# Attention and MoE in one kernel: Q and K of the first two batches loaded on 64 partitions each and transposed together

## The chip, the cores and the metric

One core of one Trainium2 chip. The metric is the device time of one execution in microseconds (us); lower is better. The engines are called PE (TensorE, the matrix unit), PEld (its weight loads), DVE (VectorE), ACT (ScalarE), POOL (GpSimd) and SP (SyncE, which here only issues DMAs). Sixteen DMA engines move data between HBM and SBUF.

## What is computed

Blockwise causal attention over 8 batches of 8 heads, 576 tokens, head size 64; its output, laid out as 4608 rows of 512, goes through a two-layer network with a swish whose steepness is learned per column. All inputs and outputs are float32.

```python
def _attn_ref(q, k, v):                     # q, k, v: (8, 8, 576, 64)
    scores = scale * np.matmul(q, k.transpose(0, 1, 3, 2))
    mask = block_i >= block_j               # blocks of 64 tokens
    scores = np.where(mask, scores, -1000000000.0)
    scores = scores - np.max(scores, axis=-1, keepdims=True)
    attn = np.exp(scores)
    attn = attn / (np.sum(attn, axis=-1, keepdims=True) + 1e-09)
    return np.matmul(attn, v)

def _moe_ref(x, w_in, w_out, beta):         # x: (4608, 512), w_in: (512, 2048), w_out: (2048, 512)
    h = x @ w_in
    g = h * (1.0 / (1.0 + np.exp(-beta * h)))
    return g @ w_out
```

## The kernel before

**Attention.** The work goes in pairs of heads, four pairs a batch; pair `u` of 32 is `b, c = divmod(u, 4)`. For a pair, Q and K are loaded as float32 into a staging tile ST, cast to bf16 into QKn, and turned so that head size lies on partitions (tile QKT: 64 partitions a head). Scores come on PE with keys on partitions (line 712), in four groups of key blocks `g0` 0 to 3: groups 0 to 2 fill two PSUM banks each and take one exponential of 128x1024 on ACT (line 728), group 3 one of 128x64 (line 740). DVE writes zeros over masked corners (734, 736). PE multiplies by V (line 768, 30 small products a pair; V carries a column of ones, so the sum of a row comes out too), DVE takes the reciprocal (780) and scales (787; for pair 1 ACT does it, line 792, in ten pieces). The result is transposed (817) and copied into xT (DVE 827, or ACT 825 for pairs 2 and 3), which is the left operand of the MoE.

**Loads of batches 0 and 1** (`b < QB`). Here Q and K of a pair are two separate loads (line 622) of 96 partitions with six tokens each: 192 pieces of 1536 bytes. There are six staging slots, so three pairs fit. Each load has a cast of its own on POOL, two of sixteen on DVE (629), six transposes of 96x128 (638) and a DVE copy out of PSUM (646). From batch 2 on other loads, casts (669) and DMA transposes (676) are used.

**V.** Batch 0's V is loaded in two halves of four heads. The first half goes by SP into a float32 tile Vs, and POOL casts it into Vn (578). Of the second half SP loads 256 tokens and POOL casts those; the other 320 tokens POOL loads itself by DMAs that cast on the way into Vn (lines 552 and 555). V of batch 1 goes whole through SP into a tile that shares its memory with OV.

**MoE.** Rows go in nine chunks of 512 (`r`). For each of 16 column blocks `j` PE forms h (line 1004, four products of 128x512), ACT takes a tanh (1014) and DVE forms the gated value gT (1018). Chunk 0 multiplies by w_out directly (1040); the others use a Strassen-like scheme (925, combined on DVE in 869 and 889, taken out in 946 and 949). w_in comes in four loads of 512 columns, w_out in four of 512 rows, all issued by POOL and cast on the way (502, 507). The first w_in waits for the K of pair 0, the other three for V of batch 0, w_out for V of batch 1.

**Order.** Nothing is ordered by hand. Every operation is declared with `P.op(engine, duration, emit, deps, tiles, prio, ...)`, and `Plan.schedule` plays the program through with these durations, gives slots of the tile classes and PSUM banks, and fixes the order on every engine by priority (lower goes first). Each engine then runs its list in that order, waiting on semaphores. A DMA has `xfer`, its time on the DMA engines in ns, and `pkt`, the time of one piece, by which two queues share. Where PE has nothing ready, filler products (443, 526) are put in. The loads by SP are chained in one sequence `seq`. `JOIN` lists batches whose pairs are scored two at a time in three visits of PE; other batches have one visit per entry of `GROUPS`.

Of the kernel before, what the change touches and what calls it, by code (L numbers as in the profile page):

```python
# [359 lines left out]
def bass_blockwise_causal_attn__then__act_swish_beta_kernel(  # L360
# [10 lines left out]
    with es:  # L371
        def sb(name, shape, dt):
            return es.enter_context(nc.sbuf_tensor(name, shape, dt))

        NQ = 2
        QB, XB, CAST = 2, 3, "POOL"
        NE = 3
        PARTS = [((0, 4, "SP", (4, 5, 0, 1, 2, 3)), (4, 8, "SP", range(2)), (4, 8, "POOL", (4, 5, 2, 3)))] + [((0, 8, "SP", range(6)),)] * 7
        GROUPS = [((0,), (1,), (2,), (3,))] + [((0, 1), (2, 3))] * 7
        NS = 6  # L380
        JOIN = (2,3,4,5,6,7)
        NO = 4
# [11 lines left out]
        QKn = [sb(f"QKn{i}", [128, 2, 2, 768], bf16) for i in range(NQ)]  # L394
        Vn = [sb(f"Vn{i}", [128, 5, 8, 66], bf16) for i in range(NQ)]
# [206 lines left out]
        xt = []  # L602
        early6 = []
        QKI, QKX = 550, 2700
        for u in range(NU):
# [8 lines left out]
            if b < QB:  # L614

                turned = []
                for w, (nm, src) in enumerate((("Q", q), ("K", k))):
                    ts, pt = P.tile("ST"), P.tile("P1")
                    early6.append(ts)
# [8 lines left out]
                    def fn(g, e, ts=ts, tn=tn, p=p, w=w):  # L628
                        return g.tensor_copy(QKn[tn.slot][0:96, p, w, :].rearrange("p (j h d) -> p j h d", j=6, h=2),  # L629
                                             ST6[ts.slot].rearrange("p h j d -> p j h d"))  # L630
# [5 lines left out]
                    def ft(g, e, tn=tn, pt=pt, p=p, w=w):  # L636
                        for i in range(6):
                            z = g.transpose(PSb[:, pt.slot, 96 * i:96 * i + 96],  # L638
                                            QKn[tn.slot][0:96, p, w, 128 * i:128 * i + 128], identB[0:96, 0:96])
                        return z  # L640

                    o = P.op("PE", 6 * 43, ft, deps=[o, c4], tiles=[tn, pt, tt_], lat=6 * 43 + 170, mode="full",
                             prio=pr(u))

                    def fc(g, e, pt=pt, td=tt_, p=p, w=w):
                        return g.tensor_copy(QKT[td.slot][:, p, w, 0:576].rearrange("c (p j) -> c p j", j=6),
                                             PSb[:, pt.slot, 0:576].rearrange("c (j p) -> c p j", j=6))
# [76 lines left out]
            for g0 in range(4):  # L724
                o, ps = qk[g0]
                if g0 < 3:
                    def fe(g, e, ps=ps, g0=g0, te=te):
                        return g.activation(E3[es_(te)][:, g0, :, :], PS[:, ps.slot:ps.slot + 2, :], ACT.Exp,  # L728
                                            scale=0.125)
                    x = P.op("ACT", act_t(1024), fe, deps=[o], tiles=[ps, te], lat=act_t(1024) + 93, prio=0)  # L730

                    def fz(g, e, g0=g0, te=te):
                        if g0 < 2:
                            return g.memset(E3[es_(te)][64:128, g0, :, 0:64], 0.0)  # L734
                        a = E3[es_(te)][64:128, 2, :, 0:64]
                        return g.memset(bass.AP(a.tensor, a.offset, [a.ap[0], [512, 2], [320, 2], [1, 64]]), 0.0)
                    zs.append(P.op("DVE", 160 if g0 < 2 else 220, fz, deps=[x], tiles=[te], prio=-20))
                else:
                    def fe(g, e, ps=ps, te=te, p=p):
                        return g.activation(E4[es_(te)][:], PS[:, ps.slot, 64 * p:64 * p + 64], ACT.Exp, scale=0.125)  # L740
                    x = P.op("ACT", act_t(64), fe, deps=[o], tiles=[ps, te], lat=act_t(64) + 93, prio=0)
                ex.append(x)
# [38 lines left out]

            r = P.op("DVE", 150, fr, deps=[av], tiles=[pv, ti], prio=0)

# [11 lines left out]

            if u in (1,):
                m = P.op("ACT", 1500, fa, deps=[av, r], tiles=[pv, ti, tx], lat=1700, prio=0)
            else:
                m = P.op("DVE", dve_t(640), fm, deps=[av, r], tiles=[pv, ti, tx], prio=0)
                m.same = [r]  # L800
# [19 lines left out]
            xp = P.op("PE", 5 * 66, fx, deps=nrm, tiles=[tx, px], lat=5 * 66 + 170, mode="full", prio=pr(u)+.5 + 5 * (b < 1))  # L820

# [21 lines left out]
        for b in range(B):  # L843
            for u in range(4 * b, 4 * b + 4):
                for o in (ld["Q", u], ld["K", u]):
                    if o not in seq:
# [287 lines left out]
```

## Time and profile before

| | us |
|---|---|
| median of three runs | 333.79 (333.38 to 335.41) |
| the profiled execution | 331.63 |
| its span, first to last instruction | 329.8 |
| PE busy in the span | 318.9 |
| DVE, ACT, POOL busy | 223.9, 212.6, 87.1 |
| granted PE clock | 1.00 |

A line of a group or timeline names the start or count, the line of the kernel, the engine, the operation and the tiles; in brackets stands how long the engine was idle before it and what released it. The span is also given in 40 slices of 8.2 us, with a digit for the busy tenths. PE's busy time includes filler.

### The profile page before, as it was taken

The numbers are of one execution on the slowest core, as the hardware profiler recorded it, in microseconds if no ns is written. First come the engines' busy times: TensorE is split into PE (matmuls) and PEld (weight loads), VectorE is DVE, ScalarE is ACT, GpSimd is POOL, SyncE is SP. The second block draws the span as 40 slices with busy tenths as digits, with TensorE's granted clock in tenths as the row PEclk, the third lists the DMA queues.
The fourth block names the chain that finished last, engine by engine and source line by source line (L and its number), as shares of the span: only waits on it lengthen the run. The fifth ranks groups of instructions, "written<-read, shape, count | busy, mean of one in ns | idle before, by whom it ended". The sixth has DMA issues, their size and how long they took to land.

```text
span 329.8 us, 7390 instructions
## 1 busy us (share of the span) xinstructions
PE 318.9 (97%) x3111; PEld 198.2 (60%) x3003; DVE 223.9 (68%) x448; ACT 212.6 (64%) x324; POOL 87.1 (26%) x127
## 2 busy tenths in 40 slices
PE   7999999999999999999999998999999999999996
PEld 1364455445687457855666655576566766666685
DVE  4848875678654899449957795678477685666742
ACT  2876974397557976678577675974876554544521
POOL 7756181065073045104530730250000000000000
PEclk9999999999999999999999999999999999999999
DMA  8999999999999999989989999969002320100023
GB/s 206 229 243 236 192 218 205 215 275 196 209 276 190 246 198 189 230 178 203 188 188 191 264 223 151 219 121 165 33 34 42 98 39 32 66 32 34 6 92 127
DMA packets 154993, 53.41 MB, mean 162 GB/s; under 512 B 139072, under 2 KB 154448, under 8 KB 154960
## 3 DMA queue, kind: packets, MB, share of 16 engines
q1 hardware_dynamic: 141200, 40.19, 64.5%
q0 software_dynamic: 5568, 4.36, 8.5%
q10 hardware_dynamic: 8192, 8.39, 8.0%
q8 instruction: 24, 0.39, 0.5%
q14 instruction: 9, 0.07, 0.1%
HBM read 36.71 MB, written 9.44 MB: 140 GB/s over the span
## 4 chain that ended last, share of the span: by engine, by line
PE 83%; ACT 4%; DVE 3%; POOL 3%; SPq 2%; DMA 2%; issue 2%; POOLq 0%; ACTq 0%
PE PS L1004 36%; PE PS L925 28%; PE PS L768 8%; PE PS L712 6%; PE PS L1040 4%; ACT E L728 3%; DMA Vs<-in_v_dram 2%; SPq L552 2%; DVE gT L1018 1%; POOL QKn L629 1%; ACT th L1014 1%; PE PS L817 1%; DVE OV L889 1%; PE PS L638 0%; POOL w_in L502 0%
## 5 line engine op out<-in xcount | busy, mean ns | idle before, releaser
L1014 ACT ACTIVATE th<-PS,beta 128x512 f32<-128x512 f32 x144 | 96.5, 700 | 60.3 <-PE PS L1004 59.1
L1004 PE MATMUL PS<-xT,w_in 128*128 128x512 bf16 x542 | 130.2, 379 | 3.7 <-ACT E L728 1.2
L1018 DVE SCALAR_TENSOR_TENSOR gT<-th,PS 128x512 f16<-128x512 f32 x144 | 95.1, 682 | 30.2 <-ACT th L1014 29.3
L728 ACT ACTIVATE E<-PS 128x1024 bf16<-128x1024 f32 x93 | 92.1, 1029 | 26.1 <-PE PS L712 25.7
L1004 PEld LDWEIGHTS PS<-xT,w_in 128*128 128x128 bf16 x576 | 53.2, 98 | 56.9 <-DVE gT L1018 2.5
L925 PE MATMUL PS<-w_out,gT 128*128 128x256 f16 x512 | 63.0, 273 | 0.0
L925 PEld LDWEIGHTS PS<-w_out,gT 128*128 128x128 f16 x512 | 49.0, 98 | 12.2 <-issue 1.5
L578 POOL CAST Vn<-Vs 128x640 bf16<-128x640 f32 (+1 forms) x28 | 22.4, 800 | 97.4 <-DMA Vs<-in_v_dram 96.1
L669 POOL CAST QKn<-ST 128x640 bf16<-128x640 f32 x48 | 37.9, 790 | 23.7 <-DMA ST<-in_q_dram 13.8
L712 PE MATMUL PS<-QKT 64*128 64x512 bf16 (+4 forms) x328 | 33.8, 295 | 0.4 <-ACT E L740 0.2
L768 PEld LDWEIGHTS PS<-Vn,E 128*128 128x128 bf16 x930 | 31.0, 97 | 4.3 <-issue 0.4
L946 ACT ACTIVATE ost<-PS 128x512 f32<-128x512 f32 x32 | 19.4, 606 | 21.7 <-PE PS L925 21.7
L925 PE MATMUL PS<-OV 128*128 128x256 f16 x256 | 32.0, 273 | 0.5 <-DVE OV L889 0.5
L768 PE MATMUL PS<-Vn,E 128*128 128x65 bf16 x930 | 32.0, 193 | 0.3 <-POOL Vn L578 0.3
L712 PEld LDWEIGHTS PS<-QKT 64*128 64x128 bf16 (+1 forms) x328 | 13.3, 96 | 27.0 <-issue 7.8
L925 PEld LDWEIGHTS PS<-OV 128*128 128x128 f16 x256 | 24.1, 98 | 6.5 <-issue 0.8
L787 DVE TENSOR_TENSOR xq<-PS,inv 128x640 bf16<-128x640 f32 x30 | 24.7, 822 | 0.8
L889 DVE TENSOR_TENSOR OV<-gT 128x1024 f16<-128x1024 f16 x32 | 24.0, 757 | 1.1 <-PE PS L925 0.6
L734 DVE MEMSET E<- 64x64 uint32 x62 | 6.9, 112 | 20.5 <-ACT E L728 18.3
L949 DVE SCALAR_TENSOR_TENSOR ost<-PS,ost 128x512 f32<-128x512 f32 x22 | 15.2, 689 | 8.2 <-PE PS L925 5.8
L925 PE MATMUL PS<-OV,gT 128*128 128x256 f16 x128 | 16.1, 273 | 0.0
L1040 PE MATMUL PS<-w_out,gT 128*128 128x512 f16 x64 | 15.5, 380 | 0.0
(64 smaller groups left out, 175.3 us busy)
## 6 DMA issues: line engine op xcount, KB each, us to landing
out_dram<-ost ACTq DMA_DIRECT2D x32, 256.0 KB, 2.9
ST<-in_q_dram SPq DMA_DIRECT2D x12, 576.0 KB, 6.2
ST<-in_k_dram SPq DMA_DIRECT2D x12, 576.0 KB, 7.6
Vs<-in_v_dram SPq DMA_DIRECT2D x24, 256.0 KB, 4.5
ST<-in_q_dram SPq DMA_DIRECT2D x8, 288.0 KB, 6.5
ST<-in_k_dram SPq DMA_DIRECT2D x8, 288.0 KB, 7.0
w_in<-in_moe_w_in_dram POOLq DMA_DIRECT2D x4, 512.0 KB, 10.1
w_out<-in_moe_w_out_dram POOLq DMA_DIRECT2D x4, 512.0 KB, 9.9
```

Of the source, the lines that this page charges most:

```text
L578: return g.tensor_copy(Vn[t.slot][:, 0:n, g0:g1, 0:64], Vs[ts.slot][:, 0:n, g0:g1, :])
L669: return g.tensor_copy(QKn[tn.slot][:].rearrange("p a w n -> p (a w n)")[:, 640 * (2 * a + w):][:, 0:640] .rearrange("p (t h d) -> p t h d ...
L712: z = g.matmul(o, QKT[tqk.slot][r, uu % 2, 1, 128 * t + y:128 * t + m + y], x)
L728: return g.activation(E3[es_(te)][:, g0, :, :], PS[:, ps.slot:ps.slot + 2, :], ACT.Exp, scale=0.125)
L768: z = g.matmul(o, eblk(te, t, i, h), Vn[Tv.slot][:, t, 2 * c + h, 0:65], start=(t == 0), stop=(t == i))
L787: return g.tensor_tensor(xq[xq_(tx)][:].rearrange("p i (h d) -> p h i d", h=2), both(pv, 0, 64), x, ALU.mult)
L889: return P.op("DVE", dve_t(SZ * HC / 2), mk(lambda g: g.tensor_tensor(fo(), fx(), fy(), op)), deps=deps, tiles=tiles, prio=prio)
L925: x = g.matmul(PS[:, pw.slot, HM * w:HM * w + HM], fa()[:, j, 128 * w:128 * w + 128], fb()[:, j, :], start=first and (pair or w == 0) and ...
L1004: z = g.matmul(PS[:, ph.slot, :], w_in[:, c, 128 * j:128 * j + 128], xT[:, c, row % RX:row % RX + RC], start=(c == 0), stop=(c == 3))
L1014: return g.activation(th[tt.slot][:], PS[:, ph.slot, :], ACT.Tanh, scale=beta[:, j:j + 1])
L1018: return g.scalar_tensor_tensor(out=gT[tg.slot][:, j, :], in0=th[tt.slot][:], scalar=1.0, in1=PS[:, ph.slot, :], op0=ALU.add, op1=ALU.mult)
L1040: z = g.matmul(PS[:, po.slot, 0:d1 - d0], gT[tg.slot][:, j, 128 * w:128 * w + 128], w_out[:, j, d0:d1], start=(j == 0), stop=(j == NJ - 1))
```

## The change

It concerns batches 0 and 1, apart from the last item.

- Q and K of a pair share one staging slot: Q on partitions 0 to 63, K on 64 to 127, nine tokens a partition, so 128 pieces of 2304 bytes a load. There are four slots, one a pair. K of pair 0 is issued by ACT, all others by SP.
- One cast covers Q and K of some token columns. For pairs 0 to 3 it is split over engines (`EARLYC`): pair 0 over DVE, ACT and POOL, the others over POOL (five of nine columns) and DVE (four). For batch 1 POOL casts all nine (1152 elements).
- A pair has nine transposes of 128x128 in two PSUM tiles (four and five) with one copy each, by DVE, except the second of pair 0 by ACT.
- All of batch 0's V comes through SP and is cast by POOL.
- The first w_in waits for K of pair 3 rather than of pair 0; the other three wait for the second half of V.
- Batch 1 joins the batches whose pairs are scored two at a time.
- DVE scales pair 1 too; some priorities of batch 0 are changed; the fifth transpose of the attention output takes 128 rows instead of 64.

```diff
-        PARTS = [((0, 4, "SP", (4, 5, 0, 1, 2, 3)), (4, 8, "SP", range(2)), (4, 8, "POOL", (4, 5, 2, 3)))] + [((0, 8, "SP", range(6)),)] * 7
+        PARTS = [((0, 4, "SP", (4, 5, 0, 1, 2, 3)), (4, 8, "SP", (4, 5, 0, 1, 2, 3)))] + [((0, 8, "SP", range(6)),)] * 7
-        NS = 6
-        JOIN = (2,3,4,5,6,7)
+        NS = 4
+        JOIN = range(1, B)
-        ST6 = [s[0:96].rearrange("p t d -> p (t d)")[:, 768 * i:768 * i + 768].rearrange("p (h j d) -> p h j d", h=2, j=6)
-               for s in ST for i in range(3)]
+        ST9 = [s[:, 18 * i:18 * i + 18].rearrange("p t d -> p (t d)") for s in ST for i in range(2)]
...
+        ACTK, QX = (0,), 745
+        EARLYC = {0: (((0, 4), 'DVE'), ((4, 7), 'ACT'), ((7, 9), 'POOL')), 1: (((0, 5), 'POOL'), ((5, 9), 'DVE')), 2: (((0, 5), 'POOL'), ((5, 9), 'DVE')), 3: (((0, 5), 'POOL'), ((5, 9), 'DVE'))}
+        LATEC = (((0, 9), 'POOL'),)
...
-                    def fl(g, e, ts=ts, src=src, b=b, c=c):
-                        return [g.dma_start(ST6[ts.slot].rearrange("p h j d -> p h (j d)"),
-                                            src[b, 2 * c:2 * c + 2].rearrange("h (p j) d -> p h (j d)", j=6))]
-                    o = ld[nm, u] = P.op("SP", 420, fl, tiles=[ts], xfer=1170, prio=u, dma=["d_S", 0, 1])
-                    o.pkt = 80.0
+                    def fl(g, e, ts=ts, src=src, b=b, c=c, w=w):
+                        return [g.dma_start(ST9[ts.slot][64 * w:64 * w + 64].rearrange("p (h n) -> p h n", h=2),
+                                            src[b, 2 * c:2 * c + 2].rearrange("h (p j) d -> p h (j d)", j=9))]
+                    e = "ACT" if w and u in ACTK else "SP"
+                    o = ld[nm, u] = P.op(e, 420, fl, tiles=[ts], xfer=QX, prio=u if e == "SP" else -80,
+                                         dma=["d_SK" if w else "d_S", 0, 1])
+                    o.pkt = 93.0
...
-                    onp = u not in (0, 3) or w == 1
-                    o = P.op("POOL" if onp else "DVE", 850 if onp else 750, fn, deps=[o], tiles=[ts, tn],
-                             prio=-40 + 3 * u if onp else -1)
+                cols = EARLYC[u] if u in EARLYC else LATEC
+                for (j0, j1), en in cols:
...
+                    n = 128 * (j1 - j0)
+                    cast[j0, j1] = P.op(en, 50 + n if en == "POOL" else 60 + 0.65 * n if en == "DVE" else act_t(n), fn, deps=got, tiles=[ts, tn],
+                                        prio=-40 + 3 * u if en == "POOL" else -1 if en == "DVE" else -60)
...
-                        for i in range(6):
-                            z = g.transpose(PSb[:, pt.slot, 96 * i:96 * i + 96],
-                                            QKn[tn.slot][0:96, p, w, 128 * i:128 * i + 128], identB[0:96, 0:96])
+                for a, (j0, j1) in enumerate(((0, 4), (4, 9))):
...
+                        for j in range(j0, j1):
+                            z = g.transpose(PSb[:, pt.slot, 128 * (j - j0):128 * (j - j0) + 128],
+                                            x[:, 128 * j:128 * j + 128], identB[:])
...
-                    turned.append(P.op("DVE", dve_t(576), fc, deps=[o], tiles=[pt, tt_], prio=-5 if b < 1 else .5))
+                    en = "ACT" if u == 0 and a else "DVE"
+                    turned.append(P.op(en, dve_t(128 * n) if en == "DVE" else act_t(128 * n), fc, deps=[o], tiles=[pt, tt_],
+                                       prio=-50 if en == "ACT" else -5 if b < 1 else .5))
...
-            if u in (1,):
+            if u in ():
                 m = P.op("ACT", 1500, fa, deps=[av, r], tiles=[pv, ti, tx], lat=1700, prio=0)
...
-                    r = 128 if i < 4 else 64
-                    z = g.transpose(PSb[:, px.slot, 128 * i:128 * i + r], xq[xq_(tx)][0:r, i, :], identB[0:r, 0:r])
+                    z = g.transpose(PSb[:, px.slot, 128 * i:128 * i + 128], xq[xq_(tx)][:, i, :], identB[:])
...
-        win[0].deps += [ld["K", 0]]
-        for o in ld["VP", 0, 4]:
-            o.deps += [ld["K", 2]]
+        win[0].deps += [ld["K", 3]]
         for w in win[1:]:
-            w.deps += ld["V", 0, 4] + (ld["VP", 0, 4] if w is not win[1] else [])
+            w.deps += ld["V", 0, 4]
```

The exponentials of batch 0 get priority -2 instead of 0, its reciprocals and scalings -6 instead of 0.

More of the change, by code (lines that the diff above doesn't have):

```diff
@@ L393, in bass_blockwise_causal_attn__then__act_swish_beta_kernel @@
         SW = {k: OVh[:, k + 1] for k in (2, 3)}
-        QKn = [sb(f"QKn{i}", [128, 2, 2, 768], bf16) for i in range(NQ)]
+        QKn = [sb(f"QKn{i}", [128, 2, 2, 640], bf16) for i in range(NQ)]
         Vn = [sb(f"Vn{i}", [128, 5, 8, 66], bf16) for i in range(NQ)]
@@ L614, in bass_blockwise_causal_attn__then__act_swish_beta_kernel @@
             if b < QB:
[L616 removed]
+                turned, got, cast = [], [], {}
+                ts, pts = P.tile("ST"), [P.tile("P1"), P.tile("P1")]
+                early6.append(ts)
                 for w, (nm, src) in enumerate((("Q", q), ("K", k))):
[L618 to L647 removed]
@@ new lines, in bass_blockwise_causal_attn__then__act_swish_beta_kernel, with fn @@
+                    o.pkt = 93.0
+                    got.append(o)
+                cols = EARLYC[u] if u in EARLYC else LATEC
+                for (j0, j1), en in cols:
+                    def fn(g, e, ts=ts, tn=tn, p=p, j0=j0, j1=j1):
+                        y = QKn[tn.slot][:].rearrange("p a w n -> p (a w n)")[:, 1152 * p:1152 * p + 1152].rearrange(
+                            "p (j h d) -> p j h d", h=2, j=9)[:, j0:j1]
+                        x = ST9[ts.slot].rearrange("p (h j d) -> p j h d", h=2, j=9)[:, j0:j1]
+                        if e == "ACT":
+                            return g.activation(y, x, ACT.Copy)
+                        return g.tensor_copy(y, x)
+                    n = 128 * (j1 - j0)
+                    cast[j0, j1] = P.op(en, 50 + n if en == "POOL" else 60 + 0.65 * n if en == "DVE" else act_t(n), fn, deps=got, tiles=[ts, tn],
+                                        prio=-40 + 3 * u if en == "POOL" else -1 if en == "DVE" else -60)
@@ new lines, in bass_blockwise_causal_attn__then__act_swish_beta_kernel, with ft, fc @@
+                for a, (j0, j1) in enumerate(((0, 4), (4, 9))):
+                    pt = pts[a]
+                    def ft(g, e, tn=tn, pt=pt, p=p, j0=j0, j1=j1):
+                        x = QKn[tn.slot][:].rearrange("p a w n -> p (a w n)")[:, 1152 * p:1152 * p + 1152]
+                        for j in range(j0, j1):
+                            z = g.transpose(PSb[:, pt.slot, 128 * (j - j0):128 * (j - j0) + 128],
+                                            x[:, 128 * j:128 * j + 128], identB[:])
+                        return z
+                    n = j1 - j0
+                    o = P.op("PE", n * 57, ft, deps=[x for (a0, a1), x in cast.items() if a0 < j1 and a1 > j0] + [c4],
+                             tiles=[tn, pt, tt_], lat=n * 57 + 170, mode="full", prio=pr(u))
+                    def fc(g, e, pt=pt, td=tt_, p=p, j0=j0, j1=j1):
+                        y = QKT[td.slot][:, p, :, 0:576].rearrange("c w (p j) -> c w p j", j=9)[:, :, :, j0:j1]
+                        x = PSb[:, pt.slot, 0:128 * (j1 - j0)].rearrange("c (j w p) -> c w p j", w=2, p=64)
+                        if e == "ACT":
+                            return g.activation(y, x, ACT.Copy)
+                        return g.tensor_copy(y, x)
@@ L729, in fe @@
                                             scale=0.125)
-                    x = P.op("ACT", act_t(1024), fe, deps=[o], tiles=[ps, te], lat=act_t(1024) + 93, prio=0)
+                    x = P.op("ACT", act_t(1024), fe, deps=[o], tiles=[ps, te], lat=act_t(1024) + 93, prio=-2 if b < 1 else 0)
                     def fz(g, e, g0=g0, te=te):
@@ L740, in fe @@
                         return g.activation(E4[es_(te)][:], PS[:, ps.slot, 64 * p:64 * p + 64], ACT.Exp, scale=0.125)
-                    x = P.op("ACT", act_t(64), fe, deps=[o], tiles=[ps, te], lat=act_t(64) + 93, prio=0)
+                    x = P.op("ACT", act_t(64), fe, deps=[o], tiles=[ps, te], lat=act_t(64) + 93, prio=-2 if b < 1 else 0)
                 ex.append(x)
@@ L780, in fr @@
                 return g.reciprocal(inv[ti.slot][:].rearrange("p (h i n) -> p h i n", h=2, n=1), both(pv, 64, 65))
-            r = P.op("DVE", 150, fr, deps=[av], tiles=[pv, ti], prio=0)
+            r = P.op("DVE", 150, fr, deps=[av], tiles=[pv, ti], prio=-6 if b < 1 else 0)
             def fm(g, e, pv=pv, ti=ti, tx=tx):
@@ L794, in fa @@
                 return z
-            if u in (1,):
+            if u in ():
                 m = P.op("ACT", 1500, fa, deps=[av, r], tiles=[pv, ti, tx], lat=1700, prio=0)
             else:
-                m = P.op("DVE", dve_t(640), fm, deps=[av, r], tiles=[pv, ti, tx], prio=0)
+                m = P.op("DVE", dve_t(640), fm, deps=[av, r], tiles=[pv, ti, tx], prio=-6 if b < 1 else 0)
                 m.same = [r]
@@ L815, in fx @@
                 for i in range(5):
-                    r = 128 if i < 4 else 64
-                    z = g.transpose(PSb[:, px.slot, 128 * i:128 * i + r], xq[xq_(tx)][0:r, i, :], identB[0:r, 0:r])
+                    z = g.transpose(PSb[:, px.slot, 128 * i:128 * i + 128], xq[xq_(tx)][:, i, :], identB[:])
                 return z
-            xp = P.op("PE", 5 * 66, fx, deps=nrm, tiles=[tx, px], lat=5 * 66 + 170, mode="full", prio=pr(u)+.5 + 5 * (b < 1))
+            xp = P.op("PE", 5 * 57, fx, deps=nrm, tiles=[tx, px], lat=5 * 57 + 170, mode="full", prio=pr(u)+.5 + 5 * (b < 1))
             def fy(g, e, px=px, c=c, b=b):
@@ L845, in bass_blockwise_causal_attn__then__act_swish_beta_kernel @@
                 for o in (ld["Q", u], ld["K", u]):
-                    if o not in seq:
+                    if o not in seq and o.engs == ("SP",):
                         seq.append(o)
```

## The prediction

> **What bounds the kernel now.** I read the page first, then the chain of waits over 0 to 60 us, the timelines of ACT, DVE, POOL and SP over the same stretch, and the DMA view in short windows. The page shows two regimes.
>
> ```profile
> span 329.8 us, 7390 instructions
> PE   7999999999999999999999998999999999999996
> PEld 1364455445687457855666655576566766666685
> DMA  8999999999999999989989999969002320100023
> ```
>
> PE counts as busy from the start, but up to 28 us much of that is filler (lines 443 and 526); PEld, low in slices 1 to 4, tells the difference. From the first MoE product (L1004, 27.9 us) to the end PE is nearly without gaps. So the time is the start of that dense part plus its length. The change touches batches 0 and 1 only: the start, and some of the next 30 us. What ends the start is in the chain of waits (start, us, what):
>
> ```profile
> 11.88 2.57 SPq L552
> 14.50 7.18 DMA Vs<-in_v_dram
> 21.73 0.41 POOL Vn L578
> 22.19 1.10 PE PS L768 x30
> 27.44 0.43 PE PS L638 x6
> 27.92 0.82 PE PS L1004 x3
> ```
>
> The last V of batch 0 lands at 21.7, then POOL casts it, PE forms P·V of pair 2 and pair 3, and the first L1004 follows. Ahead of V in the DMA engines stand Q and K of batch 0 and one quarter of w_in. The window from 2 to 11 us of the DMA view gives their rate:
>
> ```profile
> DMA packets 1709, 2.37 MB, mean 264 GB/s; under 512 B 138, under 2 KB 1709, under 8 KB 1709
> q1 hardware_dynamic: 1662, 2.33, 102.5%
> ```
>
> One load of 294,912 B costs 294,912/264e3 = 1.12 us of all sixteen engines. A second chain ends almost as late, the exponentials on ACT:
>
> ```profile
> 8.00 1.94 ACT L728 ACTIVATE E<-PS 128x1024 bf16<-128x1024 f32 x2 [5.75 <-PE PS L712]
> 20.04 1.02 ACT L728 ACTIVATE gT<-PS 128x1024 bf16<-128x1024 f32 x1 [0.18 <-PE PS L712]
> ```
>
> From 8.00 to 21.06 us ACT is hardly ever idle (13.06 us, 1.05 of it gaps). It caps what earlier loads can bring: the last exponential can't end much before 21 us.
>
> **What the Trainium skill says.** Three places bear on it.
> - "SBUF — State Buffer", Door 1: partitions 0 to 63 reach 8 of 16 DMA ports; a 1 MiB load there ran at 196 GB/s against 328 over 128 partitions, and two loads on the two halves gained 6% together. The trace of before has no large 64-partition load; its 96-partition loads run at 264 GB/s.
> - The same page, Who interferes with whom: a DVE copy in a two-port mode and a GpSimd instruction exclude each other. The trace agrees: the same DVE cast took 0.56 us alone and 1.48 beside POOL casts.
> - "ScalarE: Activation LUTs", What ACT_TABLE_LOAD costs: 186 ns + 0.833 ns per element. The trace agrees: 128x64 took 243 ns, the formula gives 239.
>
> ```profile
> 4.09 0.56 DVE L629 CAST QKn<-ST 96x768 bf16<-96x768 f32 x1 [0.82 <-DMA ST<-in_q_dram]
> 12.37 1.48 DVE L629 CAST QKn<-ST 96x768 bf16<-96x768 f32 x1
> ```
>
> **The change, part by part.**
>
> *The load itself* (the unknown that decides). 192 pieces of 1536 B on 96 partitions become 128 of 2304 B on 64. Lower bound: from the page's queues, output stores take 0.08·16·329.8 us/8192 = 51.5 ns for 1024 B, queue 1 takes 0.645·16·329.8/141200 = 24.1 ns for 285 B on average, a slope of 0.037 ns per byte, so 2304 B cost 99 ns and eight per engine 0.79 us. Upper bound: 294,912 B at the skill's 196 GB/s, 1.50 us. I take 0.80: Q goes to one half and K to the other in turn through the same engines, so both halves can be fed; the added plan writes 745 ns for it, and its old 1170 fits the measured 1.12. Neither is proof.
>
> *Batch 0.* First bytes move at about 1.9 us. Eight loads of 0.80 end at 8.3 instead of 10.9. Four slots for four pairs take away the waits of SP at 4.67 and 6.19. K of pair 0 issued by ACT puts one DMA issue (0.43 us on SP) ahead of the ACT table load; ACT is idle until 8.0, so nothing. Both halves of pair 0 land at 1.9 + 1.6 + 1.05 (the first Q: moved by 3.0, used at 4.09) = 4.6. Casts: DVE 512 columns, 0.06 + 0.65·512 = 0.39; ACT 384, 0.51 by the skill; POOL 256, 0.40 (L578 at that width) but not before its memsets end at 5.2, so 5.75. Five transposes 0.6 (six took 0.69 there), ACT's copy of 640 columns 0.60 + 128·0.833 ns = 0.71, scores 0.4, and some 0.05 for each handover: first exponential at 7.8, against 8.00. With 13.06 us of chain the last ends at 20.9.
>
> *V and w_in.* The POOL issues at 10.76 to 13.48 go (2.74 us of POOL); SP issues 12 V loads rather than 8, and Q of batch 1 stands behind them on SP, as it did. The first w_in now waits for the last K (landing 9.4) instead of the first, and its packets began 3.9 us after issue before, so from 13.3; V follows Q and K at 8.3 and needs 4608·23 ns/16 = 6.6 us alone, with the overlap between 16 and 19.5 landed; I take 18.3. Two casts of 640 columns (0.73 each, formerly 0.40) end at 19.8. So V is no longer last; the exponentials are. Pair 3's P·V can start at 21.1 instead of 23.56. From there to the last copy into xT took 3.63 us (27.19), so the first L1004 at 25.0, not 27.9: **2.9 us**. The first w_in lands by about 20.
>
> *DVE and POOL.* Copies after the transposes: 512 and 640 columns at 1.04 ns cost 0.69 + 0.82 = 1.51 us a pair, as two of 0.757. Casts of pairs 1 to 3 on DVE and POOL together: 0.39 alone, up to 1.3 if locked out; each pair has 3.3 us of exponentials as cover, so zero, at worst 1 us of ACT gaps. Normalising pair 1 on DVE (0.82) frees 2.16 us of ACT after 22.5; neither was last.
>
> *Batch 1.* The other w_in issues move to about 19.8 to 22. POOL casts a pair in 0.73 + 512·0.84 ns = 1.16 instead of 1.66 us. PE: 36 transposes of 86 ns (L817: five loads in 0.43) for 48 of 72, 0.35 us less. Six score visits for eight save two switches, about 0.2 us each. The middle visit of pairs 6 and 7 needs both E tiles, the second of which comes free only after P·V of pair 4; so pair 6's second half (1.3 us of ACT) moves behind it. That relieves ACT, which is busy 9.99 of 10 us between 30 and 40. I count **1.0 us** in all, 0 to 1.5. The V load that releases w_out landed at 41.88; sixteen loads cheaper by 0.32 are 5.1 us of DMA, so w_out is not late for a PE that is 3 to 4 us ahead.
>
> Sum: 3.9 us. The profiled execution took 331.63 (span 329.8), so 327.7; the three runs have a median of 333.79, 2.16 above it, so **329.9**.
>
> **Rivals.**
> - *The gain is given back at 46 to 58 us.* For it: the chain passes from PE through ACT there even now (51.16, one exponential), and the tile wait above puts pairs 6 and 7 one after the other behind V of batch 1, with L1040 as only cover, which needs w_out. Against: the DMAs are ahead. If 2 us are lost there: about 331.9 (331 to 333).
> - *The half-ports decide: slower.* Place: the 16 loads; price 1.40 to 1.50 us instead of 1.12. Pair 0 2.0, the rest 8.4: Q and K end at 12.3; the first w_in, issued after their landing, then cuts into V, which lands at 22.3; wider casts bring the first L1004 to 28.4, 0.5 late. Then eight more loads add 2.2, the V that releases w_out lands some 3 us later, and w_out with it: with 0.5 us, 3.6 slower, 337.4 (335 to 339). It decides from about 1.2 us a load on. For it: the skill's table. Against: alternating halves, the plan's 745.
>
> **How the numbers follow.** Forecast 0.54 (own range 328.3 to 331.5), given back 0.24, half-ports 0.22. A difference under 1% (3.3 us) can hardly be told from none here. Of the forecast 0.40 lies below 330.45 and 0.14 within 1%; given back is within, but for 0.02 faster; half-ports give 0.16 beyond 1% and 0.06 within. Faster 0.42, same 0.42, slower 0.16. Range 327.3 to 337.0: it leaves out the upper part of the half-ports and a gain over 6.5 us.
>
> **What would show it.** Right: 2304-byte pieces near 100 ns, the last K used before 10 us, last V landing by 19, pair 3's P·V waiting on ACT and not on POOL Vn, first L1004 near 25. Wrong: a DMA rate near 200 GB/s in the first 12 us; DVE casts of 1 us and gaps in the exponentials; PE idle by several us between 40 and 60 on w_out or on exponentials of pairs 6 and 7.

## The result, and the profile after

The change makes the kernel slower: 337.14 us (335.3 to 340.23) against 334.05 for the kernel before beside it, a ratio of 1.01 with a 95% interval of 1.0072 to 1.0128. Ratios below are always to the kernel before, measured beside the run in question. The forecast was 329.9 on a base of 333.79, a ratio of 0.988. The miss is thus 2.2%, some 7 us.

The page of the changed kernel first (span, busy tenths in slices of 8.3 us):

```profile
span 333.7 us, 7338 instructions
PE   5897999889999999999999999999999999999996
PEld 1354454535577557765575568755566766666685
DMA  7999999999999999997979999995030300110023
```

The span is 3.9 us longer, and the busy digits of PE don't show where; filler hides it again. The DMA view from 7 to 9.5 us, when only Q and K of batch 0 move, gives the disputed number:

```profile
DMA packets 323, 0.66 MB, mean 265 GB/s; under 512 B 35, under 2 KB 35, under 8 KB 323
q1 hardware_dynamic: 323, 0.66, 104.8%
```

265 GB/s, as before (264). A load of 294,912 B costs 1.11 us, neither my 0.80 nor the rival's 1.40 to 1.50. The larger pieces took proportionally longer. What that does at the start is in the timelines of DVE and of ACT (start, duration, line and operation, in brackets idle time before it and what ended it):

```profile
5.61 0.43 DVE L641 CAST QKn<-ST 128x512 bf16<-128x512 f32 x1 [2.34 <-DMA ST<-in_k_dram]
8.85 0.43 DVE L641 CAST QKn<-ST 128x512 bf16<-128x512 f32 x1 [2.47 <-DMA ST<-in_k_dram]
9.20 0.71 DVE L666 COPY QKT<-PS 128x512 bf16<-128x512 bf16 x1
```

```profile
11.35 1.94 ACT L749 ACTIVATE E<-PS 128x1024 bf16<-128x1024 f32 x2 [2.87 <-PE PS L733]
25.28 1.02 ACT L749 ACTIVATE gT<-PS 128x1024 bf16<-128x1024 f32 x1 [0.56 <-PE PS L733]
```

The first cast is at 5.61 instead of 4.09, since it needs both halves. Then the copy of pair 0, ready early, stands in DVE's fixed order behind the cast of pair 1, and that cast waits 2.47 us for its K. So the exponentials begin at 11.35 (8.00 before) and end at 26.3 (21.06). POOL and PE, from the same profile's timelines:

```profile
22.48 1.51 POOL L577 CAST Vn<-Vs 128x640 bf16<-128x640 f32 x2 [5.65 <-DMA Vs<-in_v_dram]
32.49 1.15 POOL L641 CAST QKn<-ST 128x1152 bf16<-128x1152 f32 x1 [1.39 <-DMA ST<-in_k_dram]
```

```profile
31.24 0.38 PE L653 MATMUL PS<-identB,QKn 128*128 128x128 bf16 x4 [0.48 <-POOL QKn L641]
33.78 0.66 PE L653 MATMUL PS<-identB,QKn 128*128 128x128 bf16 x9 [1.23 <-POOL QKn L641]
34.28 1.89 PE L1022 MATMUL PS<-xT,w_in 128*128 128x512 bf16 x8
```

V is late too (cast at 22.48; 21.73 before), and now all 36 transposes of batch 1 stand on PE ahead of the first MoE product (34.28; 27.92 before) and wait for loads of batch 1. The lateness is carried on: SP's chain of V of batch 1 ends later, and POOL may not issue w_out before it. Lines of the timelines of POOL (before, then the change) and PE (the change), then the windows view from 60 to 80 us, before and in the change (length, PE, PEld, DVE, ACT, POOL busy, clock, DMA share, GB/s):

```profile
41.88 0.75 POOL L507 DMA_DIRECT2D w_out<-in_moe_w_out_dram  x1 [6.78 <-DMA OV<-in_v_dram]
45.41 0.74 POOL L506 DMA_DIRECT2D w_out<-in_moe_w_out_dram  x1 [11.77 <-DMA OV<-in_v_dram]
63.83 1.90 PE L1058 MATMUL PS<-w_out,gT 128*128 128x512 f16 x8 [1.22 <-DMA w_out<-in_moe_w_out_dram]
70.59 0.39 PE L733 MATMUL PS<-QKT 64*128 64x512 bf16 x2 [1.13 <-DMA QKT<-QKn]
60.00:80.00 20.00, 19.89 (x127) 9.03 (x123) 15.61 (x29) 16.08 (x25) 8.80 (x11) 1.00 1.21 239
60.00:80.00 20.00, 17.66 (x146) 8.53 (x139) 12.33 (x27) 11.33 (x17) 6.11 (x8) 1.00 1.14 233
```

PE has 2.34 us of gaps there; before it had 0.11. Of these, 1.22 us are a wait for w_out and 1.13 us a wait for the first DMA transpose of batch 2, which SP issued at 59.10 (51.65 before). The chain of waits between 22 and 60 us ran through PE before; now it is SP's queue of DMA issues (pieces of 0.04 us between the first four lines left out):

```profile
22.57 4.23 SPq L551
26.84 8.03 SPq L551
34.91 4.14 SPq L551
39.09 3.31 SPq L554
...
59.10 11.44 DMA QKT<-QKn
```

An unchanged price of Q and K alone would leave w_out where it was. What did change is how much all DMA engines moved. The DMA view up to the first issue of w_out, before (0 to 41.88 us) and in the change (0 to 45.41):

```profile
DMA packets 15616, 9.25 MB, mean 221 GB/s; under 512 B 10475, under 2 KB 15611, under 8 KB 15611
DMA packets 14513, 9.39 MB, mean 207 GB/s; under 512 B 10397, under 2 KB 12461, under 8 KB 14509
```

Nearly the same bytes took 3.5 us longer. Part of that is a hole where the engines had little to do. The same view from 14 to 16 us, before and in the change:

```profile
DMA packets 2176, 0.49 MB, mean 247 GB/s; under 512 B 2158, under 2 KB 2176, under 8 KB 2176
DMA packets 787, 0.20 MB, mean 101 GB/s; under 512 B 775, under 2 KB 787, under 8 KB 787
```

The 0.29 MB missing there are some 1.2 us at 247 GB/s. The experiments show which edit the hole goes with.

### The profile page after: what moved, and what is told of

It reads as the page before. It is cut to its first block, busy times and chain, and to the rows that moved or that the text cites. A ratio compares the mean times of both kernels' runs of the same rounds, so it can differ in the third digit from the quotient of the medians.

```text
span 333.7 us, 7338 instructions
## 1 busy us (share of the span) xinstructions
PE 319.8 (96%) x3082; PEld 199.2 (60%) x2974; DVE 220.0 (66%) x450; ACT 212.4 (64%) x316; POOL 78.9 (24%) x117
## 4 chain that ended last, share of the span: by engine, by line
PE 77%; SPq 12%; DMA 5%; DVE 4%; issue 0%; ACT 0%
PE PS L1022 33%; PE PS L943 27%; SPq L551 9%; PE PS L733 7%; PE PS L789 7%; DMA QKT<-QKn 3%; DMA ST<-in_k_dram 2%; PE PS L1058 1%; SPq L554 1%; DVE gT L907 1%; SPq L679 1%; PE PS L653 1%; DVE OV L907 1%; PE PS L442 1%; SPq L623 1%; DVE w_out L887 0%
## 5 line engine op out<-in xcount | busy, mean ns | idle before, releaser
L1022 PE MATMUL PS<-xT,w_in 128*128 128x512 bf16 x576 | 135.9, 379 | 0.0
L577 POOL CAST Vn<-Vs 128x640 bf16<-128x640 f32 x28 | 20.9, 748 | 99.5 <-DMA Vs<-in_v_dram 98.2
L733 PE MATMUL PS<-QKT 64*64 64x64 bf16 (+4 forms) x328 | 34.0, 301 | 1.2 <-DMA QKT<-QKn 1.1
L907 DVE TENSOR_TENSOR OV<-gT 128x1024 f16<-128x1024 f16 x32 | 22.9, 722 | 0.9 <-PE PS L943 0.4
L755 DVE MEMSET E<- 64x64 uint32 x62 | 6.9, 112 | 22.8 <-ACT E L749 20.8
L757 DVE MEMSET E<- 64x128 uint32 x31 | 5.1, 165 | 19.2 <-ACT E L749 18.4
```

What stands on the lines that cost most here:

```text
L577: return g.tensor_copy(Vn[t.slot][:, 0:n, g0:g1, 0:64], Vs[ts.slot][:, 0:n, g0:g1, :])
L733: z = g.matmul(o, QKT[tqk.slot][r, uu % 2, 1, 128 * t + y:128 * t + m + y], x)
L907: return P.op("DVE", dve_t(SZ * HC / 2), mk(lambda g: g.tensor_tensor(fo(), fx(), fy(), op)), deps=deps, tiles=tiles, prio=prio)
L1022: z = g.matmul(PS[:, ph.slot, :], w_in[:, c, 128 * j:128 * j + 128], xT[:, c, row % RX:row % RX + RC], start=(c == 0), stop=(c == 3))
```

## Experiments

### The plan's number, and the joint visits

The plan gives 745 ns to a load that takes 1110. The first suspicion (theory A): orders made for loads that don't exist are the whole loss. Theory B: the change's structure makes the start late whatever the plan says.

```diff
-        ACTK, QX = (0,), 745
+        ACTK, QX = (0,), 1120        # first run; 930 in the second
...
-                    o.pkt = 93.0
+                    o.pkt = 140.0        # 116.0 in the second
```

> The change as it is, with one number of the plan corrected: a 64-partition load of Q or K is counted at 1120 ns (140 ns a piece) instead of 745 (93). No instruction, tile or byte differs; only the order on each engine follows another clock. Theory A (the order was made for loads that the chip does not deliver, so DVE, POOL and PE stand in fixed order behind data that is late): DVE no longer waits 2.5 us for pair 1 ahead of a copy of pair 0, the first exponential starts near 9 us instead of 11.35, and the time falls by 2 to 4 us, ratio to the kernel before 0.995 to 1.004. Theory B (the new layout itself is slower: both halves must land before any cast, and V and w_in come later): the order matters little, ratio 1.007 to 1.013 as the change measured.

> The same with 930 ns (116 a piece), half way. Theory A: between the change and the run with 1120, ratio 1.000 to 1.009, the first exponential at 9 to 11 us. Theory B: ratio 1.007 to 1.013. A third reading, that any new order is as good or bad by luck: this one and the one with 1120 scatter by some us with no relation to the number.

Measured 1.015 (1.0082 to 1.0218) and 1.0198 (1.0125 to 1.0272). With the true number the first MoE product came at 30.55, 3.7 us earlier than in the change, and the kernel was not faster; V's second half was cast at 24.16, w_out issued at 46.33. Theory A fell for the change, though both ratios lie above what theory B expected too. The mirror, the kernel before with the wrong number:

```diff
-                    o = ld[nm, u] = P.op("SP", 420, fl, tiles=[ts], xfer=1170, ...)
-                    o.pkt = 80.0
+                    o = ld[nm, u] = P.op("SP", 420, fl, tiles=[ts], xfer=745, ...)
+                    o.pkt = 62.0
```

> The converse on the kernel before: its 96-partition loads, which take 1.12 us on the chip, are counted at 745 ns (62 a piece) instead of 1170 (80). Nothing else. Theory A: it becomes slower by 1.5 to 4 us, ratio 1.004 to 1.012, with an engine of the first 15 us waiting on a load ahead of work that is ready. Theory B: ratio 0.997 to 1.003.

1.0156 (1.0102 to 1.0211): there the wrong number costs as much by itself as the whole change. It is not harmless; why its correction gained nothing in the change was not shown.

The change with batch 1 scored pair by pair:

```diff
-        JOIN = range(1, B)
+        JOIN = range(2, B)
```

> The change with batch 1 scored pair by pair again (8 visits of PE, an E tile a pair), the rest and the 745 ns as in the change. If the shared visits, which need the E tiles of two pairs, cost what is lost between 50 and 70 us, this is 1 to 3 us faster than the change (ratio to before 1.000 to 1.007). If the loss is made in the first 35 us, it stays at 1.007 to 1.014.

1.0255 (1.0194 to 1.0317), slower than either expectation. So the joint visits are no loss in the change. How much they help is not clear: in this run the granted clock was 0.50 from 35 to 40 us (1.00 in the change), and that is part of its loss.

### Every edit but the layout, on the kernel before

```diff
-        PARTS = [(..., (4, 8, "SP", range(2)), (4, 8, "POOL", (4, 5, 2, 3)))] + ...
+        PARTS = [(..., (4, 8, "SP", (4, 5, 0, 1, 2, 3)))] + ...           # V
...
-        win[0].deps += [ld["K", 0]]
+        win[0].deps += [ld["K", 3]]                                      # w_in
...
-        JOIN = (2,3,4,5,6,7)
+        JOIN = range(1, B)                                               # visits
...
-            if u in (1,):
+            if u in ():                                                  # priorities, pair 1 on DVE
```

> The kernel before with every edit of the change but the layout of Q and K: V of batch 0 all by SP, the first w_in after the last K, batch 1 scored in three visits, the priorities of exponentials and reciprocals, pair 1 scaled on DVE. Q and K stay on 96 partitions in six loads' slots with 1170 ns in the plan. Theory 'layout' (both halves needed before a cast, later issue, 0.61 us of SP per load): 331 to 333, below before, with the first exponential at 8.0 us and the first MoE product at 28 or earlier. Theory 'V and w_in' (the first w_in's pieces ahead of V, V through one queue): 336 to 338, as the change, with V's second half landing after 22 and the first MoE product at 29 to 31 although the first exponential is at 8.0.

> The kernel before with one edit of the change: batch 1 scored in three joint visits too. The change without it lost 1.5%, so if visits save switches and ACT time whatever the layout: 329 to 331 (1% faster than before). If what they gain belongs to the late loads of the change (a joint visit only hides them): 333 to 335, no difference.

> The kernel before with one edit of the change: the four V loads of batch 0 that POOL issued go to SP. Theory 'V and w_in': V's second half lands 1 to 2 us later, the first MoE product 1 to 2 us later, 335 to 336. Theory 'layout': V lands within 0.5 us of before (POOL's 2.7 us of issues are only saved), 332.5 to 334.

> The kernel before with one edit of the change: the first w_in waits for the last K of batch 0 instead of the first. If that is what puts w_in's pieces among V and batch 1's loads: V's second half no earlier than 21.7, batch 1's casts later, 334.5 to 336. If it only moves bytes in a queue that is full anyway: 332.5 to 333.8.

> The kernel before with the last part of the change that has not run alone: exponentials and reciprocals and scalings of batch 0 come earlier in the plan, and pair 1 is scaled on DVE (0.82 us) instead of ACT (2.16 us). If ACT's 2 us after 22 us count: 331 to 332. If they have cover: 332.5 to 334. If new orders cost, as other single edits of the kernel before did: 334 to 336.

| on the kernel before | ratio | interval |
|---|---|---|
| V all by SP | 1.0041 | 1.0011 to 1.007 |
| first w_in after the last K | 1.0072 | 1.0045 to 1.0098 |
| batch 1 in joint visits | 1.008 | 1.0048 to 1.0112 |
| priorities, pair 1 on DVE | 1.0003 | 0.9971 to 1.0036 |
| all four together | 1.0175 | 1.01 to 1.0249 |

The four single costs add up to 1.96%, which is near the 1.75% for all, though each is no larger than what a new order alone may cost (next section). The old layout with the other edits loses as much as the whole change, or more, and its V is late as well (POOL):

```profile
22.91 1.51 POOL L578 CAST Vn<-Vs 128x640 bf16<-128x640 f32 x2 [5.98 <-DMA Vs<-in_v_dram]
```

So no loss by the new layout is needed to make V late. But the two losses do not sit in the same place. With all four edits the DMA engines still moved 220 GB/s up to 45 us (222 before, 207 in the change), w_out was issued at 42.74, PE had no gap from 60 to 80 us, and the granted clock was 0.83 from 50 to 60 us. Equal ratios are thus no proof of an equal cause, and whether the layout gains or loses is not separated (1.01 against 1.0175, with intervals that touch).

The hole in the DMA goes with V by SP. In all eleven runs in which SP alone issues the whole of V, new layout or old, some stretch of 2 us between 9 and 20 us has only 89 to 141 GB/s: 101 in the change, 106 with V by SP on the kernel before (there w_out is issued at 43.63), 122 with all four edits. In the seven runs in which POOL issues four of these loads the lowest is 168 to 206. In the change SP's timeline has one V load that takes from 9.14 to 11.75 us to issue, and the next two, issued from 11.80 on, are of 32 KB only; that this is what empties the engines was not tested.

Two of these taught more than their ratio. In the run with joint visits alone, PE waited 0.71 us for one of DVE's copies into xT; in the run with the w_in edit, the first MoE product came at 36.0. First a line of PE's timeline in the former, then the group of line 1004 in the latter:

```profile
51.31 1.02 PE L1040 MATMUL PS<-w_out,gT 128*128 128x512 f16 x4 [0.71 <-DVE xT L827]
```

```profile
L1004 PE MATMUL PS<-xT,w_in x39: 379/379/389, 36.0 to 44.8; 128*128 128x512 bf16 x39
```

8.1 us later than before, and the kernel lost only 0.7%, 2.4 us, by it: transposes and scores of batch 1 were done ahead of the products. The time of the first MoE product is not the length of the start.

One part undone in the change: POOL issues four V loads again, after the third K.

```diff
-        PARTS = [(..., (4, 8, "SP", (4, 5, 0, 1, 2, 3)))] + ...
+        PARTS = [(..., (4, 8, "SP", range(2)), (4, 8, "POOL", (4, 5, 2, 3)))] + ...
...
+        for o in ld["VP", 0, 4]:
+            o.deps += [ld["K", 2]]
...
-            w.deps += ld["V", 0, 4]
+            w.deps += ld["V", 0, 4] + (ld["VP", 0, 4] if w is not win[1] else [])
```

> The change with one part undone: POOL again issues four of the V loads of batch 0, after the third K, and the later w_in wait for these too. Theory 'V and w_in': V's second half lands 1 to 2 us earlier than 22.5 and 1 to 2 us come back, 335 to 336. Theory 'layout': 336.5 to 338, since PE waits for the transposes of batch 1 and not for V.

1.019 (1.0134 to 1.0246), against both theories. The hole in the DMA is gone (210 GB/s from 14 to 16 us) and w_out is issued at 44.39, 1.0 us earlier than in the change. But the planner put so much of batch 1 ahead that the first MoE product came at 42.5, and from 25 to 40 us the granted clock was between 0.50 and 0.81. What costs 0.4% when added to the kernel before does not come back when taken out of the change; each edit also makes a new order, and here that order may hide what the edit is worth.

### How much is the order alone?

Two plans moved by a number that the chip never sees, the first in the kernel before, the second in the change:

```diff
-                    o = ld[nm, u] = P.op("SP", 420, fl, tiles=[ts], xfer=1170, ...)
+                    o = ld[nm, u] = P.op("SP", 420, fl, tiles=[ts], xfer=1190, ...)
...
-        ACTK, QX = (0,), 745
+        ACTK, QX = (0,), 760
```

> The kernel before with one number of the plan moved: a load of Q or K is put at 1190 ns instead of 1170. Nothing that the chip does changes but the order that the planner writes. If orders are about equally good: 332 to 334.5. If any order but this one costs what the experiments on the kernel before cost (0.4 to 1.75%): 334.5 to 338.

> The change with one number of the plan moved: a load of Q or K at 760 ns instead of 745, new orders on PE, DVE and ACT, the same work. If orders scatter: anything from 334 to 341. If the change's time is that of its work and not of its order: 336 to 338.

The kernel before: 1.0009 (0.9982 to 1.0036), though PE, DVE and ACT ran in a different order. The change with 760 ns: 1.019 (1.0133 to 1.0247), 0.9% above the change itself. So an order may be worth nothing or about 1%, and single edits of 0.4 to 0.8% can't be put down to the work that they change alone. The next runs avoid this.

### Same orders, fewer bytes

In these runs every engine keeps the instruction order of the change; only DMAs bring less. What is left out, some tokens of Q and K or half of the heads of V, is replaced by data that already lie in the tile, so these runs measure time only. Six of nine tokens make a load of 196,608 B, 0.76 to 0.81 us at the 243 to 259 GB/s measured in three of these runs (4.5 to 6.5 us), close to what I had assumed (0.80).

```diff
-                        return [g.dma_start(ST9[ts.slot][64 * w:64 * w + 64].rearrange("p (h n) -> p h n", h=2),
-                                            src[b, 2 * c:2 * c + 2].rearrange("h (p j) d -> p h (j d)", j=9))]
+                        y = ST9[ts.slot][64 * w:64 * w + 64].rearrange("p (h j d) -> p h j d", h=2, j=9); return [g.dma_start(y[:, :, 0:6] if b < 1 else y,
+                                            src[b, 2 * c:2 * c + 2].rearrange("h (p j) d -> p h j d", j=9)[:, :, 0:6] if b < 1 else src[b, 2 * c:2 * c + 2].rearrange("h (p j) d -> p h j d", j=9))]
...
-                        x = ST9[ts.slot].rearrange("p (h j d) -> p j h d", h=2, j=9)[:, j0:j1]
+                        f = 3 if j1 > 6 and j1 - j0 < 9 else 0; x = ST9[ts.slot].rearrange("p (h j d) -> p j h d", h=2, j=9)[:, j0 - f:j1 - f]
```

This is "batch 0 short"; "batch 1 short" has the condition the other way round and leaves the casts as they are. For half of V:

```diff
-                        d = Vn[t.slot] if e == "POOL" else Vs[ts.slot]
+                        d = Vn[t.slot] if e == "POOL" else Vs[ts.slot]; H = h0 + 2 if b < 1 else h1
...
-                            return [g.dma_start(d[:, i, h0:h1, 0:64],
-                                                v[b, h0:h1, 128 * i:128 * i + 128, :].rearrange("h p d -> p h d"))]
+                            return [g.dma_start(d[:, i, h0:H, 0:64],
+                                                v[b, h0:H, 128 * i:128 * i + 128, :].rearrange("h p d -> p h d"))]
...
```

> The change with every engine's order as it is, but each load of Q or K of batch 0 brings six of the nine tokens of a partition (196,608 B, about 0.75 us at 264 GB/s, what the plan assumes); the casts read three tokens twice, so scores of batch 0 are wrong by that. Theory 'load term' (the 0.80 us I forecast for a load that takes 1.11 is the failed term; all else follows): first exponential 8 to 9, last V landed by 20, first MoE product 26 to 28, time 329 to 332. Theory 'structure' (both halves needed, 0.61 us of SP a load, V and w_in later, joint visits): at most 1.5 us come back, 335 to 337.

> As the run before, same orders, and each V load of batch 0 brings two heads of its four (half of V's bytes; the casts read them twice). If V of batch 0 then bounds the start: another 1 to 2 us less than the run before. If it doesn't (SP's issues, POOL's casts of batch 1 and PE's fixed order bound it): within 0.5 us of the run before.

> The change with every engine's order as it is, but each load of Q or K of batch 1 brings six of the nine tokens of a partition (the other three keep what the slot held). Theory 'order and late loads' (all 36 transposes of batch 1 stand ahead of the first MoE product on PE and wait for POOL's casts of loads that land at 27.5 to 32.5): casts 1 to 3 us earlier, the first MoE product at 31.5 to 33 instead of 34.3, 335 to 336. If V of batch 0 (cast at 22.5, P.V of pair 3 at 27.2) sets the start: 0 to 0.5 us less than the change.

> The change with every engine's order as it is, and each V load of batch 0 brings two heads of its four (half of V's bytes, 0.59 MB or 2.2 us at 264 GB/s; the casts read them twice); loads of Q and K whole. If V ahead of batch 1's loads and of w_in is a term of its own: V's second half cast at about 20.3, 2 us back, 335. If it counts only once the loads of batch 0 are short: at most 0.7 us back.

> The change with every engine's order as it is, each load of Q or K of batches 0 and 1 brings six of nine tokens (196,608 B; the other three are read twice in batch 0 and keep what the slot held in batch 1). If the load price and the late loads of batch 1 make up the early loss: the exponentials of batch 0 end at about 21.5, POOL's four casts of batch 1 run from about 23.2 without a wait, the first MoE product at 28 to 29.5 instead of 34.3, 330 to 332. If V of batch 0 is the term that remains (the run with half of V alone gave 331.9): first MoE product no earlier than 30.5, 332.5 to 334.

For the run with both batches short, batch 1 fetches the last six tokens of a partition, not the first. All times in us, from the timelines of each run:

| | exponentials of batch 0 | V's second half cast | batch 1 cast by | first MoE product | first w_out issued | ratio (interval) |
|---|---|---|---|---|---|---|
| before | 8.00 to 21.06 | 21.73 | 35.1 | 27.92 | 41.88 | 1 |
| change | 11.35 to 26.3 | 22.48 | 33.6 | 34.28 | 45.41 | 1.01 (1.0072 to 1.0128) |
| batch 1 short | 10.86 to 26.1 | 22.82 | 31.3 | 32.63 | 43.23 | 1.0053 (1.0023 to 1.0083) |
| batch 0 short | 9.05 to 22.7 | 19.41 | 32.8 | 34.26 | 43.33 | 1.0043 (1.002 to 1.0066) |
| both short | 8.97 to 22.9 | 18.54 | 30.3 | 31.04 | 40.12 | 0.9958 (0.9931 to 0.9985) |
| half of V | 10.65 to 25.2 | done by 18.4 | 31.3 | 32.20 | 41.32 | 0.9988 (0.9951 to 1.0025) |
| batch 0 short, half of V | 9.24 to 22.8 | 17.79 | 30.3 | 31.73 | 41.55 | 0.9967 (0.994 to 0.9994) |

In "batch 0 short" the exponentials end 3.6 us earlier, the first MoE product stays at 34.26, where 26 to 28 had been expected, and 0.6% come back all the same. The lines of PE and the window of 60 to 80 us of that run:

```profile
29.85 0.58 PE L653 MATMUL PS<-identB,QKn 128*128 128x128 bf16 x4 [1.84 <-POOL QKn L641]
34.26 2.60 PE L1022 MATMUL PS<-xT,w_in 128*128 128x512 bf16 x7 [0.22 <-DVE QKT L666]
60.00:80.00 20.00, 19.23 (x188) 10.07 (x185) 12.82 (x29) 12.61 (x21) 6.96 (x10) 1.00 1.11 228
```

What came earlier at the start was spent on waiting for batch 1's loads, and on the clock: PE's granted clock was 0.50 from 30 to 35 us here, and 0.66 in the other two runs with a short batch 0, but 1.00 in the change, in "batch 1 short" and in "half of V". So the ratios of these three runs hold a cost that the others don't have. The gain is further on: w_out is issued 2.1 us earlier, and PE has 1.57 us less of gaps between 60 and 80 us (19.23 busy against 17.66). With both batches short (POOL, then PE, then the same window):

```profile
29.13 1.15 POOL L641 CAST QKn<-ST 128x1152 bf16<-128x1152 f32 x1 [3.35 <-DMA ST<-in_k_dram]
30.42 0.82 PE L653 MATMUL PS<-identB,QKn 128*128 128x128 bf16 x9 [1.90 <-POOL QKn L641]
31.04 3.45 PE L1022 MATMUL PS<-xT,w_in 128*128 128x512 bf16 x8
60.00:80.00 20.00, 20.00 (x171) 10.12 (x166) 15.52 (x33) 14.47 (x23) 9.57 (x12) 1.00 1.09 236
```

No gap is left between 60 and 80 us, and the time is 330.92, within what was expected; the first MoE product (31.04) is later than expected (28 to 29.5), since the last pair of batch 1 still waits 3.35 us for its K, whose transfer shares the DMA engines with the three w_in loads that POOL issued from 19.98 on. Half of V alone does nearly as much, and more than either reading expected (335 or more): it leaves the loads of batch 0 as slow as they are, but lets POOL finish V by 18.4, everything behind it in the queue moves up, and the hole in the DMA is gone (220 GB/s from 14 to 16 us; with batch 0 short as well there is one again, 52 GB/s from 11 to 13). So these bytes count wherever they are, which is what a start bound by DMA looks like. The order of the ratios follows w_out's issue roughly, 1.4% for 5.3 us from the change to "both short"; that w_out alone carries it was not isolated.

### Only the plan of batch 1's loads corrected

```diff
-                    o = ld[nm, u] = P.op(e, 420, fl, tiles=[ts], xfer=QX, ...)
+                    o = ld[nm, u] = P.op(e, 420, fl, tiles=[ts], xfer=QX if b < 1 else 1500, ...)
```

> The change with one number of the plan: loads of Q and K of batch 1 at 1500 ns (they landed 1.2 to 1.5 us apart in the change), those of batch 0 still at 745. Half of batch 1's transposes then stand behind the first 20 MoE products on PE. Theory 'order and late loads': the first MoE product at 29.5 to 31.5, 2 to 3 us back, 334 to 335.5. If what is saved there is only put off (scores of batch 1 later, exponentials late): 336 to 338.

337.51 (334.25 to 340.17, four runs) against 332.57; they scatter too much for an interval, and there is no sign of the 2 to 3 us. Half of the transposes now stood behind the first products, which began at 31.26; w_out was issued at 45.56, as in the change. This fits the second reading, that a new order of PE without fewer bytes only puts the wait off, but four scattered runs don't prove it.

## Why the prediction was wrong

**The load's price, the term that failed.** I took 0.80 us, near the lower bound, from a slope between two average pieces, an argument on feeding both halves, and the plan's 745. It measured 1.11, the rate of the kernel before. Same orders with loads of about the assumed price give 0.9958 instead of 1.01: 1.4%, or 4.7 us (intervals combined: about 3.4 to 6.0), of a miss of 7.2. What I had at hand was better: the measured 264 GB/s on 96 partitions. The slope was no evidence: it compared stores of 1024 B with a queue full of pieces of 285 B, in other stages and directions.

**What followed from it.** V landed after 22 instead of 18.3, the exponentials ended at 26.3 instead of 20.9. The step "w_out is not late" rested on the same 0.32 us times sixteen. With a load of the assumed price V was cast at 18.54, w_out was issued at 40.12 and the gaps from 60 to 80 us were gone: these steps were right given their premise.

**A term that was missing.** Without the gain on loads w_out should have come as before, at 41.88. It came 3.5 us later, and up to there the DMA engines moved 207 GB/s instead of 221. The forecast had no term for this. The hole from 14 to 16 us, which goes with V by SP, is an estimated 1.2 us of it (above); the first bytes, at about 2.2 us instead of 1.75, are some 0.4; the rest was not traced. The lateness then cost PE 1.22 us at w_out and 1.13 us at the first transpose of batch 2.

**The first exponential.** Even with the short loads it came at 8.97 and not at 7.8. The first cast was at 4.93 (forecast 4.6); the rest is DVE's order, where the copy of pair 0 (6.82) stands behind the cast of pair 1 (6.47, itself 0.87 waiting for K). "Zero, at worst 1 us" for these casts looked at their duration, not at what they wait for and who stands behind. Part of the late first bytes is SP: issuing one of the new loads took 0.61 us instead of 0.44 (medians of the groups of lines 623 and 622), which I had put at the old price.

**The conversion into time.** "First L1004 at 25.0, not 27.9: 2.9 us" was more than its own sum gives, since P·V of pair 3 was to move by 2.46 us (from 23.56 to 21.1). And it took the start of the MoE products as the end of the start. The w_in run shows that it can move by 8.1 us for 2.4. The planner moves work across that mark; what counts is how much of PE's work is done by a given time. I had also not asked what the new orders would put ahead of it: all 36 transposes, waiting for batch 1's loads.

**The edits costed at nothing or as gains.** V by SP, the w_in wait and the joint visits I put at 0, 0 and up to +1.0 us of gain. On the kernel before they cost 0.4, 0.7 and 0.8%. In the change the run without joint visits was 1.5% slower, as forecast in sign, but its clock fell. V by SP comes with the hole in the DMA, so it was not free. How much of the single costs is the work and how much a less lucky order stays open; the forecast held no term for the order at all. The pair 1 edit, put at nothing, measured nothing.

**The rivals.** The half-port rival named the right time (337.4) for a wrong reason, so by luck: the page "SBUF — State Buffer" of the Trainium skill, Door 1, gives 196 GB/s for a load on one half, but with loads to the two halves in turn no loss showed (265 GB/s), so the bound of 1.2 us a load from which it was to decide was never reached. Its other steps, later V, w_out some 3 us late, did happen, at an unchanged price. Of "given back at 46 to 58 us" the place was nearly right (60 to 80), the resource (w_out) was one that I had cleared. Casts and copies came as worked out: POOL's 1152 columns 1.15 to 1.18 us (1.16), ACT's copy 0.77 (0.71), DVE's cast 0.43 (0.39); only POOL's part of pair 0, 0.65 (0.40), and its 640 columns beside a DVE cast, 0.97 (0.73), took longer. One reading of the kernel before was not right: beside the DVE cast of 1.48 us POOL was issuing DMAs, from 11.94 to 13.48, and cast only from 13.46 on. In the change DVE's casts beside a cast of POOL took 0.43, the last 0.55, so the 1.3 us feared did not come.

**Still open:** the other 2.5 us of the miss (0.9883 against 0.9958) are not split between DVE's order, batch 1's late last load, the fallen clock of that run (0.66 from 30 to 35 us) and the side edits. No version with all of its data loaded was faster than the kernel before.

## What to carry to other kernels

Price a reshaped transfer at the rate that the trace shows for the nearest transfer, not from a slope between unlike ones, and when a queue is full, count bytes before you count instructions. Check also that the queue stays full: compare what the DMA engines moved up to the same event, before and after. In a kernel whose orders a planner writes, test a cause with the orders held fixed (fewer bytes, the same instructions), and measure once what a change of the plan alone is worth. The start of the next stage's first instruction is a mark that a planner can move at will; ask instead how much work of the bounding engine is still to come.

## What the runs showed of the hardware

- Loads on 64 partitions, halves in turn, pieces of 2304 B, ran at 265 GB/s; 96 partitions with 1536 B ran at 264; 64 partitions with 1536 B, in the short runs, at 243 to 259 over windows of 2 us. Among these, neither the piece nor the half made a difference beyond that scatter.
- Issuing a load of 64 partitions with two pieces each took SP 0.61 us, one of 96 partitions with two pieces 0.44. Fewer pieces (128 against 192) did not make the issue shorter.
- When SP alone issued the twelve V loads of batch 0, the DMA engines fell to 89 to 141 GB/s over some 2 us before 18 us, in eleven runs of eleven; with POOL issuing four of them the lowest was 168 to 206, in seven of seven.
- After a stretch with PE much idle, the granted clock could fall for a while. From 20 to 40 us of "batch 0 short" (columns as above):

```profile
20.00:30.00 10.00, 5.91 (x111) 4.29 (x102) 5.94 (x15) 3.23 (x6) 6.47 (x8) 0.96 1.09 229
30.00:40.00 10.00, 8.91 (x55) 4.32 (x52) 5.03 (x10) 5.70 (x9) 1.15 (x1) 0.69 1.22 211
```

  Seven MoE products took 2.60 us there (34.26, above), against 1.67 for the seven in "batch 1 short". In the change itself PE was busy for only 2.46 us from 5 to 10 us, and the clock stayed at 1.00. So the busy share alone does not tell when it falls, and that idleness is the cause was not tested.
